# The left-over tokens' part of K^T V from two half tiles of 64 rows instead of one zero-padded tile of 128 rows

## The chip, the cores and the metric

The kernel runs on one core of a Trainium2 chip. The metric is the device time of one execution in microseconds (us). Four runs of the kernel before gave a median of 770.48 us (769.99 to 773.08). One execution was profiled: it took 770.82 us, of which 769.0 lie between the first and the last instruction of the program (the span).

The engines are named as in the profile: PE is TensorE's matmuls, PEld its weight loads, DVE is VectorE, ACT is ScalarE, POOL is GpSimd, SP is SyncE, which only issues transfers here. A q behind a name (SPq) is the engine's sequencer.

## The reference

A linear attention without softmax, a normalization, and a feed-forward block with a product of two projections, in float32:

```python
# q, k, v: (batch 8, heads 8, tokens 576, head_dim 64)
kv = np.einsum('bhsd,bhse->bhde', k, v)          # 64 x 64 for each batch and head
out = np.einsum('bhsd,bhde->bhse', q, kv)
rms = np.sqrt(np.mean(out * out, axis=-1, keepdims=True) + 1e-06)
x = (out / rms * g_norm)                          # then to (4608 tokens, 512)
a, b = x @ w1, x @ w2                             # 512 -> 1024 each
y = ((a * b) @ w3) @ w_out                        # 1024 -> 1024 -> 512
```

The change is in the first line alone: kv of one batch and head is a sum over 576 tokens.

## The kernel before

**Tokens.** 576 is four times 128 and 64 more. The kernel calls the 512 tokens G (J = 4 slices of P = 128) and the 64 tokens left over L. The 512 of each batch make one group of rows for the feed-forward block; the left-over tokens of all eight batches (8 x 64 = 512) make a ninth, so there are nine groups of 512 tokens.

**The stages.** First (about the first 88 us) the weights are read, converted, and w3 and w_out are folded into one matrix (L596 are the products of this, L583 the transposes), while the attention of batch 0 runs in between, one pair of heads at a time. Then nine groups follow: the gate products x@w1 and x@w2 (`gates`, Winograd's scheme with seven products, L617), and the output projection (`project` for the first group; `project_twice`, two levels of the scheme, L892, for the others). The attention of batch T+1 is spread over the gate products of group T: `winograd` calls `between()` twice for each of four blocks, so eight slots in a group, and `steps(b)` says what runs in each slot.

**Attention of a batch.** Heads are taken in pairs r = 0 to 3, heads 2r and 2r+1 (e = 0, 1). `kv(rs)` multiplies K^T and V for the pairs in rs. The result of head e lies on the PSUM partitions 64e to 64e+63 of one bank (`kv_ps`), 64 columns for each pair. For each pair there are J + 1 = 5 slices of the token sum: four of 128 tokens from the tiles `k_sb` and `v_sb`, and a fifth from the left-over tiles `kl_sb` and `vl_sb`. Each slice is two products (L326), one for each head, of 128 rows and 64 columns against 64 columns. A float32 product leaves two matmul records in the trace. Four copies of ACT (L337) then bring the bank to `kv_sb`, each head's block once to either half of the partitions. `product(h)` (L409) multiplies the queries of the pairs 2h and 2h+1 with kv: 32 products of 64 rows and 64 columns, with the row half (l) as the innermost loop and the column half (t) around it. `product_left` (L427) does the same for the left-over queries. `q_t` (L345) transposes queries on TensorE, in batch 0 and part of batch 1; later `q_by_dma` does it with transfers and POOL copies (L286, L288, L298).

**The left-over tiles.** `kv_left` holds two tiles, each of 128 partitions by 8 heads by 64. `load_kv_left(b)` (L105) fills partitions 0 to 63 with the 64 left-over tokens of batch b, one transfer each for k and v; partitions 64 to 127 are set to zero by POOL once, at the start (L250), and stay zero. There is one buffer: the rows of batch b+1 are loaded after the last pair of batch b has been multiplied.

**The order.** PE, POOL and SP issue in the order of the program text all the time (`manual_schedule`). DVE and ACT also do in the first stage, and DVE in the double projections; elsewhere their order is the framework's choice, by its own estimate of when each instruction is ready. SP's queue carries nearly all transfers, in order; a transfer whose buffer is still in use holds up those behind it. Transfers count on eight semaphores in turn, and one that takes a semaphore again waits for the transfer before it on the same one.

**Where it is called.** In batch 0, `begin(r)` runs `kv([r])` and `q_t(r)` for one pair in a block of the second half of the fold, four calls. For the other batches `begin_kv(0, 1)` and `begin_kv(2, 3)` run two pairs in one call, 14 calls:

```python
fs[1] += [(a.begin_kv, 2, 3), (a.finish, 0)]              # finish(h) runs product(h)
fs[second].append((batch(b + 1).begin_kv, 0, 1))
fs[second].append((a.finish, 1))
```

In batch 1 the call for pairs 0 and 1 is followed by `begin_q`, that is by L345. `begin_kv` issues after the products the loads of k and v two pairs ahead (`load_ahead`), and, behind those of the last pair, `load_kv_left(b + 1)`.

Of the kernel before, what the change touches and what calls it, by code (L numbers as in the profile page):

```python
# [11 lines left out]
FP32 = mybir.dt.float32  # L12
# [9 lines left out]
def kernel(  # L22
# [32 lines left out]
    nc = tc.nc  # L55
    PSUM = bass.MemoryType.PSUM
    P = 128

    B, H, S, D = q.shape
# [5 lines left out]
    J = 4  # L65
    G = J * P
    N = G // 2
    L = S - G
# [3 lines left out]
    const = ctx.enter_context(tc.tile_pool(name="const", bufs=1))  # L72
# [9 lines left out]
    def bank(pool, tag):  # L82
        return pool.tile([P, 512], FP32, name=tag, tag=tag)


    loaded = {}
    q_left = {}

    kv_left = [const.tile([P, H, D], FP32, name=f"{name}l_sb") for name in "kv"]

    def load_pair(names, b, r):

# [9 lines left out]

    def load_kv_left(b):
        for t, src in zip(kv_left, (k, v)):
            nc.sync.dma_start(out=t[0:L], in_=src[b, :, G:S, :].rearrange("h p d -> p h d"))  # L105

    def load_q_left(b):
        if b % 2 == 0:
# [137 lines left out]

    ident = const.tile([P, P], FP32, name="ident")
    make_identity(nc, ident)
    for t in kv_left:
        nc.gpsimd.memset(t[L:P], 0.0)  # L250
    eps_col = const.tile([P, 1], FP32, name="eps_col")
    nc.vector.memset(eps_col, 1e-6)

# [54 lines left out]
    def attention(b):  # L308
# [6 lines left out]
        def kv(rs):  # L315


            n = len(rs)
            kv_ps = bank(ps_at, "at")[:, 0:n * D].rearrange("p (r d) -> p r d", d=D)
            for r in rs:  # L320
                k_sb, v_sb = loaded["k", b, r], loaded["v", b, r]
                kl, vl = kv_left
                for j in range(J + 1):
                    cols = slice(j * D, (j + 1) * D)
                    for e in range(2):
                        nc.tensor.matmul(  # L326
                            kv_ps[e * D:(e + 1) * D, r - rs[0], :],
                            lhsT=k_sb[:, e, cols] if j < J else kl[:, 2 * r + e, :],
                            rhs=v_sb[:, e, cols] if j < J else vl[:, 2 * r + e, :],
                            start=(j == 0),  # L330
                            stop=(j == J),
                        )
            for e in range(2):
                for i in range(2):
                    dst = kv_b[i * D:(i + 1) * D, e, rs[0]:rs[0] + n, :]
                    src = kv_ps[e * D:(e + 1) * D]
                    nc.scalar.copy(dst, src)  # L337
# [130 lines left out]
        def load_ahead(names, r):  # L468

            if r + 2 < NP:  # L470
                load_pair(names, b, r + 2)
            elif b + 1 < B:
                load_pair(names, b + 1, r + 2 - NP)
                if r + 1 == NP and "k" in names:
                    load_kv_left(b + 1)

        def begin_kv(*rs):
            kv(rs)
            for r in rs:
                load_ahead("kv", r)  # L480
# [527 lines left out]
    with tc.manual_schedule(  # L1008
# [6 lines left out]
        for e in range(2):  # L1015
            nc.scalar.dma_start(
                out=g_row[:, e * D:(e + 1) * D], in_=g_norm.rearrange("(o d) -> o d", o=1)
# [13 lines left out]
        for c in range(KF):  # L1031

            if c == 0:
                end_next()
                begin_next()
            else:
                begin_next()
                end_next()
            if c == 4:
                load_kv_left(0)  # L1040
                load_pair("kvq", 0, 0)
            elif c == 5:
                load_pair("kvq", 0, 1)
                load_q_left(0)
            fold_chunk(0, c, range(NH - 1))
            turn_w3(*((0, c + 1) if c + 1 < KF else (1, 0)))
            fold_chunk(0, c, [NH - 1])
            if c == 0:
                keep_warm(4)
# [123 lines left out]
```

## Time and profile before

| what | value |
|---|---|
| median of four runs | 770.48 us |
| the profiled execution | 770.82 us, span 769.0 us |
| kv (L326) | 640 records, of them 128 from the left-over tiles |
| L409 and L427 | 1024 and 128 records |
| transfers | 132.55 MB, mean 172 GB/s |
| zeroing of the left-over tiles (L250) | 0.52 us for each of two |
| issue of the left-over tiles (L105) | 16 transfers, median 0.62 us each for k and 0.63 for v |

How to read the profile: the page gives busy time by engine, the share of each engine in the chain of work that ended last, and groups of instructions by line, "out<-in", shape, count, busy time, mean ns and the idle time before them. A matmul's own duration (222 ns for L326) is its way through the array; matmuls overlap, so what a group of them costs is read from starts, or from the chain in order of time, where each piece lasts until the next begins.

### The profile page before, as it was taken

The numbers are of one execution on the slowest core, as the hardware profiler recorded it, in microseconds if no ns is written. First come the engines' busy times: TensorE is split into PE (matmuls) and PEld (weight loads), VectorE is DVE, ScalarE is ACT, GpSimd is POOL, SyncE is SP. The second block draws the span as 40 slices with busy tenths as digits, with TensorE's granted clock in tenths as the row PEclk, the third lists the DMA queues.
The fourth block names the chain that finished last, engine by engine and source line by source line (L and its number), as shares of the span: only waits on it lengthen the run. The fifth ranks groups of instructions, "written<-read, shape, count | busy, mean of one in ns | idle before, by whom it ended". The sixth has DMA issues, their size and how long they took to land.

```text
span 769.0 us, 14423 instructions
## 1 busy us (share of the span) xinstructions
PE 759.1 (99%) x5775; PEld 659.3 (86%) x5775; DVE 543.0 (71%) x1087; ACT 249.9 (32%) x483; POOL 134.9 (18%) x132
## 2 busy tenths in 40 slices
PE   7999999999999999999999999999999999999997
PEld 5455788888899889988998899889988998898897
DVE  7978999438978577756775777658665863594566
ACT  6687743213322232223213322332233222212221
POOL 0000000122610451133114511340144000000000
PEclk9999999999999999999999999999999999999999
DMA  9995641338997854874486548744843460074015
GB/s 316 338 346 171 211 138 42 83 92 256 325 305 250 233 109 129 270 199 110 128 280 176 124 139 285 180 109 146 279 70 43 159 233 0 1 244 146 1 52 175
DMA packets 132776, 132.55 MB, mean 172 GB/s; under 512 B 76645, under 2 KB 120677, under 8 KB 132709
## 3 DMA queue, kind: packets, MB, share of 16 engines
q1 hardware_dynamic: 130256, 116.81, 52.3%
q10 hardware_dynamic: 2452, 14.81, 5.7%
q8 instruction: 46, 0.75, 0.4%
q14 instruction: 22, 0.17, 0.1%
HBM read 100.27 MB, written 16.38 MB: 152 GB/s over the span
## 4 chain that ended last, share of the span: by engine, by line
PE 93%; DMA 4%; ACT 2%; DVE 1%; issue 0%; SPq 0%; DVEq 0%; ACTq 0%
PE mm L617 60%; PE mm L892 21%; PE mm L596 6%; PE at L326 3%; PE at L409 2%; DMA raw<-in_moe_w_dram 1%; DMA raw<-in_moe_w_out_dram 1%; DMA raw<-w3o_l 1%; PE at L583 1%; PE at L345 0%; ACT ab L152 0%; ACT w_sb L153 0%; PE at L427 0%; DMA out_dram<-raw 0%; ACT w3o_sb L601 0%; PE at L442 0%
## 5 line engine op out<-in xcount | busy, mean ns | idle before, releaser
L617 PE MATMUL mm<-xT,w_sb 128*128 128x256 f32 x768 | 176.2, 379 | 0.0
L617 PEld LDWEIGHTS mm<-xT,w_sb 128*128 128x128 f32 x768 | 145.5, 190 | 19.9 <-issue 0.5
L617 PE MATMUL mm<-xc,ws 128*128 128x256 f32 x576 | 130.5, 379 | 0.3 <-ACT p L630 0.3
L617 PEld LDWEIGHTS mm<-xc,ws 128*128 128x128 f32 x576 | 109.4, 190 | 15.5 <-ACT p L630 0.7
L756 DVE TENSOR_TENSOR c<-mm,u 128x512 f32<-128x512 f32 x36 | 24.8, 689 | 105.7 <-PE mm L617 105.7
L630 ACT COPY u<-mm 128x512 f32<-128x512 f32 x74 | 43.3, 585 | 139.0 <-PE mm L617 128.8
L630 ACT COPY p<-mm 128x512 f32<-128x512 f32 x74 | 43.3, 586 | 84.5 <-PE mm L617 78.5
L617 PE MATMUL mm<-xc,w_sb 128*128 128x256 f32 x288 | 69.3, 383 | 0.0
L892 PE MATMUL mm<-w3o_sb,raw 128*128 128x128 f32 x500 | 62.3, 276 | 0.0
L596 PE MATMUL mm<-chunks,ab 128*128 128x512 f32 x128 | 60.2, 601 | 1.9 <-ACT chunks L153 1.3
L617 PE MATMUL mm<-xT,ws 128*128 128x256 f32 x256 | 61.1, 382 | 0.0
L284 POOL COPY xT<-xn 128x1024 uint16<-128x1024 uint16 x26 | 32.2, 1265 | 160.2 <-DVE xn L387 160.1
L617 PEld LDWEIGHTS mm<-xc,w_sb 128*128 128x128 f32 x288 | 53.7, 190 | 7.7 <-ACT u L630 0.2
L757 DVE TENSOR_TENSOR ab<-c 128x256 f32<-128x256 f32 x108 | 58.0, 537 | 3.0
L892 PEld LDWEIGHTS mm<-w3o_sb,raw 128*128 128x128 f32 x500 | 59.0, 192 | 0.1
L617 PEld LDWEIGHTS mm<-xT,ws 128*128 128x128 f32 x256 | 48.0, 190 | 6.6
L378 DVE TENSOR_REDUCE inv<-sq 128x8 f32<-128x512 f32 (+1 forms) x40 | 23.4, 625 | 35.2 <-ACT sq L377 35.2
L756 DVE TENSOR_TENSOR c<-p,u 128x512 f32<-128x512 f32 x36 | 28.2, 783 | 27.9 <-ACT u L630 27.7
L892 PE MATMUL mm<-w3o_sb,ab 128*128 128x128 f32 x336 | 43.7, 275 | 0.0
L903 ACT COPY u<-mm 128x512 f32<-128x512 f32 x23 | 13.5, 586 | 87.5 <-DVE raw L916 56.7
L596 PEld LDWEIGHTS mm<-chunks,ab 128*128 128x128 f32 x128 | 21.9, 190 | 22.9 <-issue 15.8
L892 PEld LDWEIGHTS mm<-w3o_sb,ab 128*128 128x128 f32 x336 | 41.0, 192 | 0.3
(157 smaller groups left out, 1135.0 us busy)
## 6 DMA issues: line engine op xcount, KB each, us to landing
w3o_sb<-w3o_l SPq DMA_DIRECT2D x26, 896.0 KB, 5.0
raw<-in_moe_w_dram SPq DMA_DIRECT2D x31, 512.0 KB, 7.3
raw<-w3o_l SPq DMA_DIRECT2D x13, 896.0 KB, 4.8
w3o_sb<-w3o_l ACTq DMA_DIRECT2D x11, 896.0 KB, 4.6
k_sb<-in_k_dram SPq DMA_DIRECT2D x32, 256.0 KB, 3.9
v_sb<-in_v_dram SPq DMA_DIRECT2D x32, 256.0 KB, 4.7
q_sb<-in_q_dram SPq DMA_DIRECT2D x32, 256.0 KB, 4.4
out_dram<-raw SPq DMA_DIRECT2D x14, 512.0 KB, 3.6
```

The costliest lines, as they stand in the source:

```text
L284: nc.gpsimd.tensor_copy(to, src.rearrange("p a n w -> p w a n"))
L326: nc.tensor.matmul(kv_ps[e * D:(e + 1) * D, r - rs[0], :], lhsT=k_sb[:, e, cols] if j < J else kl[:, 2 * r + e, :], rhs=v_sb[:, e, cols] i ...
L378: nc.vector.tensor_reduce(out=inv[:, i], in_=sq.rearrange("p (h d) -> p h d", d=D), axis=AX.X, op=ALU.add)
L409: nc.tensor.matmul(o_ps[l][tokens, n * D:(n + 1) * D], lhsT=qT[r][rows, e, i, tokens], rhs=kv_b[rows, e, r, :], start=True, stop=True,)
L583: nc.tensor.transpose(t_ps[:, m, :], src, ident)
L596: nc.tensor.matmul(sums_ps[half][m], lhsT=w3T[half, c][:, m, :], rhs=chunks[:, c, 1, :], start=(c == 0), stop=(c == KF - 1),)
L617: nc.tensor.matmul(ps[:, u, :], lhsT=lhsT(a_name, u, c), rhs=rhs(b_name, c),  start=(u == 0 and c == 0 and to is None), stop=(c == chunks ...
L630: nc.scalar.copy(t, ps)
L756: nc.vector.tensor_add(c, one, two)
L757: nc.vector.tensor_mul(dst, c[:, 0, :], c[:, 1, :])
L892: nc.tensor.matmul(to[:, i, :], lhsT=x[:, c, :], rhs=y[:, c, :], start=new and place // 4 not in seen, stop=(c == 1), skip_group_check=True,)
L903: nc.scalar.copy(t[:, 0:4], ps[0])
```

## The change

The left-over tiles get 4 heads instead of 8 in each partition: heads 0 to 3 (pairs 0 and 1) lie on partitions 0 to 63, heads 4 to 7 (pairs 2 and 3) on partitions 64 to 127. Nothing is zero, so the two memsets go. `load_kv_left` issues two transfers for each of k and v, one for each half. The products of the left-over tokens use 64 rows instead of 128: both heads of a pair, and both pairs of a call, take the same half of the rows. In `kv` all slices of 128 tokens of all pairs of the call come first, then the left-over products of all pairs. The start flag of the accumulation is set only for the first pair's first slice (for each head) instead of for each pair's first slice, and the stop flag on the left-over products.

```diff
-    kv_left = [const.tile([P, H, D], FP32, name=f"{name}l_sb") for name in "kv"]
+    kv_left = [const.tile([P, H // 2, D], FP32, name=f"{name}l_sb") for name in "kv"]
...
     def load_kv_left(b):
         for t, src in zip(kv_left, (k, v)):
-            nc.sync.dma_start(out=t[0:L], in_=src[b, :, G:S, :].rearrange("h p d -> p h d"))
+            for i in range(2):
+                heads = src[b, i * H // 2:(i + 1) * H // 2, G:S, :]
+                nc.sync.dma_start(out=t[i * L:(i + 1) * L], in_=heads.rearrange("h p d -> p h d"))
...
-    for t in kv_left:
-        nc.gpsimd.memset(t[L:P], 0.0)
...
+            def add(r, e, k_in, v_in, start, stop):
+                nc.tensor.matmul(
+                    kv_ps[e * D:(e + 1) * D, r - rs[0], :], lhsT=k_in, rhs=v_in,
+                    start=start, stop=stop, skip_group_check=True,
+                )
+
             for r in rs:
-                k_sb, v_sb = loaded["k", b, r], loaded["v", b, r]
-                kl, vl = kv_left
-                for j in range(J + 1):
-                    cols = slice(j * D, (j + 1) * D)
+                for j in range(J):
                     for e in range(2):
-                        nc.tensor.matmul(
-                            kv_ps[e * D:(e + 1) * D, r - rs[0], :],
-                            lhsT=k_sb[:, e, cols] if j < J else kl[:, 2 * r + e, :],
-                            rhs=v_sb[:, e, cols] if j < J else vl[:, 2 * r + e, :],
-                            start=(j == 0),
-                            stop=(j == J),
-                        )
+                        k_in, v_in = (loaded[name, b, r][:, e, j * D:(j + 1) * D] for name in "kv")
+
+                        add(r, e, k_in, v_in, r == rs[0] and j == 0, False)
+
+            for r in rs:
+                rows = slice(r // 2 * L, (r // 2 + 1) * L)
+                for e in range(2):
+                    k_in, v_in = (t[rows, r % 2 * 2 + e, :] for t in kv_left)
+                    add(r, e, k_in, v_in, False, True)
```

## The prediction

> **What bounds the kernel now.** First the shares of the page, then the chain of work that ended last, because the bound of a stage is what ends last there.
>
> ```profile
> PE 759.1 (99%) x5775; PEld 659.3 (86%) x5775; DVE 543.0 (71%) x1087; ACT 249.9 (32%) x483; POOL 134.9 (18%) x132
> ...
> PE 93%; DMA 4%; ACT 2%; DVE 1%; issue 0%; SPq 0%; DVEq 0%; ACTq 0%
> ```
>
> TensorE is busy for 99% of the span and carries 93% of the chain; its granted clock reads 9 tenths or more in all 40 slices. Other work costs time only where TensorE waits for it. So the question is how long TensorE needs for the changed products, and whether anything else becomes late. The chain in order of time gives that (start, length, what; x counts records, and one float32 product leaves two):
>
> ```profile
> 64.30 0.73 PE at L326 x20
> 65.03 0.59 PE at L345 x4
> ...
> 69.49 0.76 PE at L326 x20
> 70.25 0.02 issue
> 70.27 0.20 ACT kv_sb L337
> ...
> 102.17 1.32 PE at L326 x40
> 103.49 1.02 PE at L345 x8
> 104.51 5.18 PE mm L617 x24
> ...
> 138.70 1.31 PE at L326 x40
> 140.02 1.09 PE at L409 x64
> ...
> 153.39 0.62 PE at L427 x32
> ...
> 178.39 1.32 PE at L326 x40
> ...
> 199.99 1.31 PE at L326 x40
> 201.30 1.09 PE at L409 x64
> 202.39 19.19 PE mm L617 x88
> ```
>
> L326 is kv. 20 records take 0.73 us and 40 take 1.31, so one record costs 0.029 us and a group pays 0.15 us beyond its records (0.73 - 20 x 0.029). L409 and L427 are the 64x64 products with kv: 64 records take 1.09 and 32 take 0.62, which is 0.0147 us a record, again with 0.15 fixed. L345, the 128x128 transposes after kv: (1.02 - 0.59)/4 = 0.11 a record, 0.15 fixed. L617 has 0.2158 a record where no other shape stood just before (5.18/24); behind L409, 88 records take 19.19 instead of 18.99, so 0.20 fixed. I read the fixed part as what a change of tile shape costs, 0.15 to 0.20 us each. Then the shapes themselves and the left-over rows:
>
> ```profile
> L326 PE MATMUL at<-v_sb,k_sb 128*64 128x64 f32 x512 | 20.6, 226 | 0.0
> L409 PE MATMUL at<-kv_sb,qT 64*64 64x64 f32 x1024 | 18.6, 221 | 0.0
> ...
> L326 PE MATMUL at<-vl_sb,kl_sb 128*64 128x64 f32 x128 | 9.2, 222 | 0.0
> ```
>
> The last line is what the change remakes: 128 records of 128 rows by 64 columns, half of the rows zero. At 0.029 they are 3.7 us of the span, the most that the edit of the products could ever save.
>
> **The change part by part.** The sum is made against the profiled execution: 769.0 us of span and 1.8 around it, 770.82, which is 0.34 above the median 770.48 of the four runs.
>
> *Products of the left-over rows.* Still 128 records, now 64 rows by 64 columns. In a call of kv both pairs of heads use the same half of the rows (pairs 0 and 1 the lower, 2 and 3 the upper); only the two heads of a pair lie in different column halves. The trace has no such group, so I bound it. L409 puts four tiles side by side (two row halves by two column halves) at 0.0147 a record, which is 4 records per 0.0587 us; kv now puts two column halves side by side, 2 records per 0.058. The new group has two tiles, as kv has, so I take 0.029 a record: no gain. From below: the rate of L409, 128 x (0.029 - 0.0147) = 1.8 us saved. From above: the two tiles after each other, 0.058 a record, 128 x 0.029 = 3.7 us lost.
>
> The Trainium skill, TensorEngine Tiling (Array Packing), section Performance Considerations, asks for row tiling where the contraction is at most 64, and its Overview puts the speedup at up to 2x. By that the 128 records would cost 1.85 us less and the sum would end about 1.0 us below the time before. The same page's Key Properties says that changing the tiling mode drains TensorE, which speaks against the change and agrees with the 0.15 to 0.20 us above.
>
> *Changes of shape.* In 13 of the 18 calls of kv, all from 109.69 on, kv is followed by L409, as at 138.70 and 199.99. There the order 128x128, 128x64, 64x64, 128x128 stays; the change to 64x64 only moves ahead of the left-over products. Nothing is added. In batch 0 the four calls run one pair each, and kv is followed by the 128x128 transposes L345 (at 47.80, 52.99, 64.30 and 69.49); so it is at 102.17. Five calls get one change of shape more: 0.15 us into 64x64, and 0 to 0.05 more on the way back (0.20 instead of 0.15). That is 0.75 to 0.95 us, all on the chain: the chain stays on TensorE from 15.66 to 70.25, and at 70.27 the chain goes on through the kv copies, which wait for the last left-over product. I take +0.85. From below it is 0, if the fixed part belongs to the 128-row shapes alone; L427, 64x64 right behind L617 with the same 0.15, speaks against that.
>
> *Order inside kv.* The left-over products of the first pair now wait for the second pair's k and v too; these landed long before (issued a half batch ahead), and the copies to kv_sb wait for the whole bank in both versions. Nothing. A call now waits for its own half of the left-over rows: two landings per call instead of two per batch. The calls at 178.39 and 199.99, without and with such a wait, took 1.32 and 1.31, so the waits cost nothing.
>
> *Transfers.* Each batch issues four transfers for the left-over rows instead of two, each with half the pieces and the same bytes in all. First the view of the tile (ns, least/median/most of one issue), then SP's rows in order of time:
>
> ```profile
> L105 SPq DMA_DIRECT2D kl_sb<-in_k_dram x8: 607/616/749, 27.5 to 484.8; - x8
> ```
>
> ```profile
> 70.15 0.37 SPq L95 DMA_DIRECT2D k_sb<-in_k_dram  x1
> ...
> 71.13 0.62 SPq L105 DMA_DIRECT2D kl_sb<-in_k_dram  x1
> 71.80 0.63 SPq L105 DMA_DIRECT2D vl_sb<-in_v_dram  x1
> ```
>
> 512 pieces (64 rows by 8 heads) take SP 0.62 us, the 256 of k_sb 0.37. A half has 256 pieces: 0.37. So SP works 4 x 0.37 + 2 x 0.05 - 2 x 0.62, about 0.35 us more per batch; from above, with 0.62 for a half, 1.3 us; from below nothing. Behind it on SP's queue: once (73.85) the loads of the last weights, else the transposes of q for the pairs 2 and 3. Those had landed at 193.5 in the batch around 200, POOL had qT ready at 195.4, and TensorE read it at 201.23: 5.8 us to spare. The left-over rows themselves landed at 191.25 and are read from 199.99 on: 8.7 us to spare. The weight loads are on the chain: issued from 73.85 on, they land at 82.17, 83.68, 85.13, 86.48, 87.84, every 1.4 us, while SP issues the first ones 0.5 to 0.6 apart. They queue behind data, not behind SP, so I cost the later issue at nothing; without that cover it is 0.35, at most 1.3.
>
> The Trainium skill, DMA: Bandwidth & Descriptors, Rules for kernel authors, advises against two transfers to disjoint halves of the partitions, since both are spread over the same engines, and says that under 64 KB one pays mostly overhead; a half here is 64 KB. With the page's fixed 2.0 us for each of the 16 added transfers on the path it would be an estimate of 32 us more; the slack above says that they are not on the path.
>
> *The two memsets* of POOL go (0.52 us each, at 1.0 and 1.96). One stands between the two steps that build the identity, so the warm-up matmuls start up to 0.5 us earlier. The chain begins with weight transfers and ACT until 15.66, so nothing comes of it.
>
> Sum: +0.85, from the median 770.48 to 771.3. With the issue time on the chain and its upper price, 0.95 + 1.3, it would be 772.7; with no change of shape paid, 770.5. A measurement of this kernel can tell about 0.3% (2.3 us) from no change: 768.2 to 772.8 is the same.
>
> **The rivals.**
>
> *The planner sets another order (slower).* From the first gate product on, the order on DVE and ACT is not written out but chosen by the framework from its own estimates of when each instruction is ready. Other products and more transfers can swap neighbours. For it: DVE is at 9 tenths from 77 to 134 us, and TensorE once already waits for a bank (at 88.02, 0.28 us, its weight load 0.68, for the copy p of L630). Against it: that is nearly the only such wait, five banks buffer, and nothing that DVE or ACT do is changed. One such wait of 0.28 to 0.68 in each of nine groups is 2.5 to 6.1; with 0.37, 3.3, so 774.6. It decides from about four of the longer ones.
>
> *The two heads of a pair don't run side by side on half of the rows (slower).* At L326's left-over records, +3.7: 775.0 with the changes of shape. It decides once a record takes more than 0.040 us (1.45 us more than the sum). Against it: L409's four tiles include two that share rows.
>
> *The left-over products run beside L409 (faster).* They share the shape now, and L409 also uses the other row half. Fully hidden they give 3.7 - 0.85 = 2.85 us, 767.6; at L409's rate 1.0, so 769.5. Against it: L409 keeps both halves busy in turn, so a half that is taken by kv delays it by as much.
>
> *Nothing moves*: the extra shape changes hide behind the weights' transfers of the first 88 us: 770.5.
>
> **How the numbers follow.** As summed 0.48 (own range 770.4 to 772.7); nothing moves 0.05; beside L409 0.08, of which 0.05 is below 768.2; planner 0.31; not side by side 0.08. Faster 0.05, same 0.48 + 0.05 + 0.03 = 0.56, slower 0.39. The range goes from 769.3 (below it lies the deeper part of the faster case, some 0.06) to 775.3 (above it a part of the planner's, some 0.09).
>
> **What would show it.** Right: the chain's L326 groups as x32 with x8 of the left-over tile at 0.03 us a record; the group before L409 at 1.3 us with L409 at about 0.95 (its fixed part moved into L326), their sum 2.40 as now; the calls of batch 0 longer by 0.15 to 0.20; L105 sixteen times per tensor at about 0.37; TensorE's idle time unchanged. Wrong: a sum of 2.3 or 2.6 there; new idle time of TensorE before L617 with DVE or ACT as releaser; weights that land later than 82 us by more than TensorE's own delay.

## The result and the profile after

The changed kernel takes 772.13 us (median of 51 runs; 770.36 for 79 runs of the kernel before, measured beside it). The medians differ by 1.77 us. The ratio of the two over all these runs is 1.0019, with a 95% interval of 1.0013 to 1.0025, or 1.46 us more (1.0 to 1.9); this is the figure used below. By the bound of 0.3% this is the same; the interval leaves no doubt that it is a little slower. The profiled execution has a span of 770.1 us (769.0 before).

The page of the kernel after, busy time of the engines and their shares of the chain of work that ended last:

```profile
PE 760.8 (99%) x5775; PEld 660.6 (86%) x5775; DVE 542.4 (70%) x1087; ACT 249.7 (32%) x483; POOL 134.0 (17%) x130
...
PE 96%; DMA 2%; DVE 1%; ACT 1%; issue 0%; SPq 0%; DVEq 0%; ACTq 0%
```

The same number of matmul records, TensorE still the bound, two POOL instructions fewer (the memsets). The chain in order of time (start, length, what); all line numbers have moved (kv by minus five, the others by plus five), so kv is now L321, the transposes behind it L350, the products with kv L414, the gate products L622 and their copies L635:

```profile
65.37 0.88 PE at L321 x20
66.25 0.59 PE at L350 x4
...
87.39 1.06 ACT w3o_sb L606 x2
88.46 1.05 ACT w_sb L155
89.50 0.48 ACT p L635
...
90.03 14.21 PE mm L622 x64
104.24 1.46 PE at L321 x40
...
202.12 1.39 PE at L321 x37
203.51 0.06 PE at L414 x2
...
203.58 0.93 PE at L414 x62
204.51 19.19 PE mm L622 x88
```

Three things can be read here. A call of batch 0 takes 0.88 us instead of 0.73, and the call of batch 1 that stands in front of transposes 1.46 instead of 1.32. In the steady state kv and L414 together go from 202.12 to 204.51, 2.39 us, where they took 2.40 (199.99 to 202.39): nothing. And in front of the gate product at 90.03 the chain runs over ACT, from 87.39 on. In the kernel before it had left TensorE at this place too, and for longer, from 70.27 to 88.02, by way of SP's issue of the last weights and their transfer (before):

```profile
73.90 0.52 SPq L190
...
74.48 7.69 DMA raw<-in_moe_w_dram
...
82.25 1.16 ACT ab L152
...
87.49 0.48 ACT p L630
...
88.02 14.15 PE mm L617 x64
```

So already before the change SP's issue of these weights stood on the way to the gate product at 88.02.

I set every matmul record of this trace against the record of the same number in the trace of before; the difference of their starts (the offset) shows where time comes in. From the first record of kv to the first one behind kv, or behind L409 where that follows, it grows by this much (us; the times are those of before):

| kernel | 48 | 53 | 64 | 69 | 102 | 110 | each of the 12 calls from 139 on |
|---|---|---|---|---|---|---|---|
| changed | 0.14 | 0.15 | 0.14 | 0.14 | 0.14 | -0.06 | -0.01 to -0.02 |

The calls of batch 0 and the one at 102 sum to 0.71, the 13 others to -0.2: there the offset rises by 0.15 at the first left-over record and falls again at the first record of L414. Apart from the calls it jumps by 0.65 at the gate product that starts at 90.03. Together 1.2, inside the measured 1.0 to 1.9. Three more steps are in the trace, +0.75 by 15.66 us, +0.3 between 222 and 240, and -1.08 at 687. The first and the last are landings of weights that differ between executions: the twelve later profiles stand between -0.2 and +0.6 at 15.66, and all but one of them win the same 1.08 at 687, where the profile of before had waited 0.9 us for a transfer. The step at 222 to 240 is as large in the kernel with the order alone changed (+0.34, third experiment below), which ends no slower than the kernel before.

What comes late at 90 us starts on SP. The timeline of the kernel after (start, length, engine, line, operation, in brackets the idle time ahead and what ended it):

```profile
72.30 1.30 SPq L107 DMA_DIRECT2D kl_sb<-in_k_dram  x2
73.64 1.27 SPq L107 DMA_DIRECT2D vl_sb<-in_v_dram  x2
...
76.31 12.14 SPq L192 DMA_DIRECT2D raw<-in_moe_w_dram  x8
...
84.34 1.13 ACT L154 ACTIVATE ab<-raw 128x1024 f32<-128x1024 uint32 x1 [1.45 <-DMA raw<-in_moe_w_dram]
...
90.03 1.99 PE L622 MATMUL mm<-xc,ws 128*128 128x256 f32 x8 [0.93 <-ACT p L635]
```

The four transfers occupy SP for 2.61 us (72.30 to 74.91) where two took 1.30. The weights' loads start at 76.31 instead of 73.85, the second one lands at 84.26 instead of 82.17, and ACT, which works in order, waits 1.45 us for it (0.72 before). The copy p that TensorE needs stands behind three such conversions. TensorE waits 0.93 us for it instead of 0.28.

The left-over products by shape, and the issues of one left-over tile (ns: least, median, most):

```profile
L321 PE MATMUL at<-vl_sb,kl_sb 64*64 64x64 f32 x128 | 7.6, 232 | 0.0
...
L107 SPq DMA_DIRECT2D kl_sb<-in_k_dram x16: 595/602/755, 28.6 to 487.9; - x16
```

A half tile takes SP 0.60 us, as long as the whole one did (0.62).

### The profile page after: what moved, and what is told of

The parts are those of the page before. It is cut to its first block, busy times and chain, and to the rows that moved or that the text cites. A ratio compares the mean times of both kernels' runs of the same rounds, so it can differ in the third digit from the quotient of the medians.

```text
span 770.1 us, 14435 instructions
## 1 busy us (share of the span) xinstructions
PE 760.8 (99%) x5775; PEld 660.6 (86%) x5775; DVE 542.4 (70%) x1087; ACT 249.7 (32%) x483; POOL 134.0 (17%) x130
## 4 chain that ended last, share of the span: by engine, by line
PE 96%; DMA 2%; DVE 1%; ACT 1%; issue 0%; SPq 0%; DVEq 0%; ACTq 0%
PE mm L622 60%; PE mm L897 22%; PE mm L601 7%; PE at L321 3%; PE at L414 2%; DMA raw<-in_moe_w_out_dram 1%; PE at L588 1%; PE at L350 1%; DMA raw<-in_moe_w_dram 0%; PE at L447 0%; PE at L432 0%; DMA out_dram<-raw 0%; ACT ab L154 0%; DVE raw L921 0%; ACT w3o_sb L606 0%; ACT w_sb L155 0%
## 5 line engine op out<-in xcount | busy, mean ns | idle before, releaser
L622 PE MATMUL mm<-xT,w_sb 128*128 128x256 f32 x768 | 176.2, 379 | 0.0
L622 PEld LDWEIGHTS mm<-xT,w_sb 128*128 128x128 f32 x768 | 145.5, 190 | 19.9 <-issue 0.5
L622 PE MATMUL mm<-xc,ws 128*128 128x256 f32 x576 | 130.5, 379 | 0.9 <-ACT p L635 0.9
L622 PEld LDWEIGHTS mm<-xc,ws 128*128 128x128 f32 x576 | 109.4, 190 | 16.1 <-ACT p L635 1.3
L635 ACT COPY u<-mm 128x512 f32<-128x512 f32 x74 | 43.3, 586 | 137.9 <-PE mm L622 131.0
L635 ACT COPY p<-mm 128x512 f32<-128x512 f32 x74 | 43.3, 585 | 84.5 <-PE mm L622 81.1
L622 PE MATMUL mm<-xc,w_sb 128*128 128x256 f32 x288 | 69.3, 383 | 0.0
L622 PE MATMUL mm<-xT,ws 128*128 128x256 f32 x256 | 61.1, 382 | 0.0
L622 PEld LDWEIGHTS mm<-xc,w_sb 128*128 128x128 f32 x288 | 53.7, 190 | 7.8 <-ACT u L635 0.3
L622 PEld LDWEIGHTS mm<-xT,ws 128*128 128x128 f32 x256 | 48.0, 190 | 6.6
L761 DVE TENSOR_TENSOR c<-p,u 128x512 f32<-128x512 f32 x36 | 26.5, 735 | 27.1 <-ACT u L635 27.1
```

The costliest lines, as they stand in the source:

```text
L622: nc.tensor.matmul(ps[:, u, :], lhsT=lhsT(a_name, u, c), rhs=rhs(b_name, c),  start=(u == 0 and c == 0 and to is None), stop=(c == chunks ...
L635: nc.scalar.copy(t, ps)
L761: nc.vector.tensor_add(c, one, two)
```

## The experiments

The theory after this reading: 0.71 us are five changes of tile shape, 0.65 are SP's time in front of the last weights, the rest of the change is free. The rivals: that the products themselves or their order cost, that weights wait for data and not for SP, and that the framework's order on DVE and ACT has shifted. The last one needed no run: the instructions on ACT and on DVE of the two compiled kernels follow each other in the same order, one by one.

### Transfers alone, products alone

The kernel before with four transfers, everything else untouched:

```diff
-            nc.sync.dma_start(out=t[0:L], in_=src[b, :, G:S, :].rearrange("h p d -> p h d"))
+            for i in range(2):
+                heads = src[b, i * H // 2:(i + 1) * H // 2, G:S, :]
+                nc.sync.dma_start(
+                    out=t[0:L, i * H // 2:(i + 1) * H // 2, :], in_=heads.rearrange("h p d -> p h d")
+                )
```

> The kernel before, with one change: the left-over rows of k and v come in two transfers each (heads 0 to 3, heads 4 to 7) instead of one. Products, zeros and memsets stay. Theory (transfers make the last weights late): a half takes SP about 0.60 us to issue, so SP is 1.2 to 1.3 us later at the loads of the last weights (73.85 in the kernel before); they land 0.7 to 1.3 us later than in the kernel before, TensorE waits longer before the gate products that begin at 88.02, and the whole is 0.5 to 0.9 us longer (ratio about 1.0009). Rival (the weights queue behind data, not behind SP, as predicted): landing unchanged, ratio 1.0000 within its interval.

Measured: 1.0010 (0.9995 to 1.0024). The halves take 0.60 to 0.61 us; the weights' loads start at 75.28 instead of 73.85, the second lands at 82.94 instead of 82.17, and the offset of the matmul records grows by 0.51 at 88.02 and at no call of kv. The trace says what was expected; the interval alone would not decide.

The changed kernel with the two transfers and the zeros of before; all heads stay on partitions 0 to 63:

```diff
-                    k_in, v_in = (t[rows, r % 2 * 2 + e, :] for t in kv_left)
+                    k_in, v_in = (t[0:L, 2 * r + e, :] for t in kv_left)
```

> The changed kernel, with the two transfers and the memsets of the kernel before: all eight heads' left-over rows on partitions 0 to 63, and all left-over products on those 64 rows; order and shapes as in the changed kernel. Theory: only the five added changes of shape remain, 5 x 0.145 = 0.7 us, ratio about 1.0009; the groups of kv in batch 0 take 0.88 instead of 0.73 us, the weights land as in the kernel before plus TensorE's own delay of up to 0.6. Rival (the wait before 90.03 in the changed kernel comes from the products, not from the transfers): about +1.4 us, ratio 1.0018, as the changed kernel.

Measured: 1.0012 (1.0004 to 1.0021). The offset grows by 0.14 to 0.15 at each of the five calls in front of transposes and by nothing at the others, as in the changed kernel, and at 88.02 it falls by 0.44 instead of growing, for here the weights landed early (80.89). The interval alone still holds the rival's 1.0018; the trace has no wait at 88. So the two parts cost about as much each, and the wait at 88 belongs to the transfers; how firmly, the comparison of all profiles below tells.

### Is it the order inside a call?

The kernel before with the changed loops alone (all slices of 128 tokens first, then the left-over products, still 128 rows with zeros):

```diff
-                    k_in, v_in = (t[rows, r % 2 * 2 + e, :] for t in kv_left)
+                    k_in, v_in = (t[:, 2 * r + e, :] for t in kv_left)
```

> The kernel before with the changed order of the products alone: in a call all slices of 128 tokens of all pairs first, then the left-over products of all pairs, still of 128 rows with zeros, from the tiles and transfers of before. Theory (the order costs nothing): no offset at any call of kv, ratio 1.0000, taken as 0.9995 to 1.0005. Rival (part of what the 64-row products seemed to cost in the run with the products alone is the order, which makes the first pair's last products wait): some 0.14 us at each of the calls of batch 0 or at each two-pair call, 0.6 to 2 us, ratio 1.0008 to 1.0026.

Measured: 0.9997 (0.9988 to 1.0006). The offset grows by 0.00 at 17 of the 18 calls (-0.04 at 110). The order is free.

### What does a change of shape cost?

The kernel before with 64 rows in place, behind each pair's own slices:

```diff
-                            lhsT=k_sb[:, e, cols] if j < J else kl[:, 2 * r + e, :],
-                            rhs=v_sb[:, e, cols] if j < J else vl[:, 2 * r + e, :],
+                            lhsT=k_sb[:, e, cols] if j < J else kl[0:L, 2 * r + e, :],
+                            rhs=v_sb[:, e, cols] if j < J else vl[0:L, 2 * r + e, :],
```

> The kernel before, with the left-over products reading 64 rows, but left where they stand: behind each pair's own four slices, so that a call of two pairs goes 128x64, 64x64, 128x64, 64x64. Same tiles, same two transfers per batch, zeros kept and not read. Theory (a change of shape costs 0.145 us, whatever stands around it): 13 calls in front of L409 get two changes more each (3.77), the call at 102 three (0.44), the four calls of batch 0 one each (0.58): 4.8 us, ratio 1.0062, taken as 1.0055 to 1.0070. Rival (the 0.145 us seen at the first left-over record are not the change of shape but a cost of the 64-row products, which ends as soon as other 64-row products follow): the same 128 records in the same calls, 0.7 to 1.5 us, ratio 1.0009 to 1.0020.

Measured: 1.0055 (1.0042 to 1.0068); 4.6 us between the medians. The chain of this kernel at the call that took 1.31 + 1.09 before:

```profile
201.51 1.70 PE at L326 x38
...
203.26 0.93 PE at L409 x61
204.20 1.93 PE mm L617 x8
```

From 201.51 to 204.20 are 2.69 us instead of 2.40: two changes of shape more, 0.145 each. The offset grows by 0.14 to 0.15 in each call of batch 0, by 0.44 at 102 and by 0.28 at each of the 12 calls from 139 on. So it is the change that costs, not the 64-row product, and the price is the same in every place.

### Does the steady state pay?

The change from batch 2 on; batches 0 and 1 keep tiles, zeros, two transfers and 128 rows:

```diff
+                    if b < 2:
+                        k_in, v_in = (t[:, 2 * r + e, :] for t in kv_left)
+                    else:
+                        k_in, v_in = (t[rows, r % 2 * 2 + e, :] for t in kv_left)
```

> The change from batch 2 on alone. Batches 0 and 1 have the left-over rows as before (two transfers, 128 rows, the zeros written at the start), in the changed order of the products; batches 2 to 7 have four transfers of half tiles and 64-row products on either half of the rows. Theory (the whole cost lies in the five calls in front of the transposes and in batch 1's transfers in front of the last weights; in the steady state the change of shape only moves and the transfers are hidden): +0.15 us in kv and -0.15 us in L409 at each call from 125 us on, ratio 1.0000, taken as 0.9995 to 1.0004. Rival (each batch pays something that two profiles can't show): 12 of the 18 calls carry two thirds of the 1.46 us, ratio 1.0013.

Measured: 1.0006 (0.9990 to 1.0023), medians 770.36 and 770.49. The interval is too wide to shut out the rival. The trace does it for the calls: over each of the 12 changed ones the offset moves by -0.01 to -0.02, and TensorE waits for none of the left-over tiles. One wait is new, 0.66 us at 469 us for weights of the output projection (`w3o_sb`). The changed kernel has no such wait there, and kernels with two transfers have one like it at 546 to 549 us (0.56 to 0.76), so it can't be put down to the change.

### Does SP stand in front of the weights?

More transfers in this one place alone, in the kernel before:

```diff
+            cuts = [0, 3, 6, H] if b == 1 else [0, H]
+            for i, j in zip(cuts, cuts[1:]):
+                hs = slice(i, j)
+                nc.sync.dma_start(out=t[0:L, hs], in_=src[b, hs, G:S, :].rearrange("h p d -> p h d"))
```

> The kernel before, with the left-over rows of batch 1 alone brought by six transfers instead of two (three for each tensor: 3, 3 and 2 heads, all to partitions 0 to 63). All products and all other batches are as before. At 0.60 us an issue, SP reaches the last weights' loads 2.4 us later: first issue at about 76.3 instead of 73.85, as in the changed kernel, but with TensorE itself not late. Theory (SP's issue time stands in front of the weights, and they on the chain): the second load lands at about 84.3 instead of 82.17, and the gate products at 88.02 start 1.3 to 1.9 us later, because nothing else has used up the slack; nothing more after that. Ratio 1.0017 to 1.0025. Rival (the prediction's cover: the weights queue behind data, not behind SP): landing of the later weights unchanged, ratio 1.0000.

Measured: 1.0027 (1.0016 to 1.0038). SP in this kernel, and what TensorE waited for (us in total, times, longest):

```profile
71.03 1.98 SPq L108 DMA_DIRECT2D kl_sb<-in_k_dram  x3
73.05 1.91 SPq L108 DMA_DIRECT2D vl_sb<-in_v_dram  x3
...
76.37 11.40 SPq L193 DMA_DIRECT2D raw<-in_moe_w_dram  x8
...
PE mm L620 <- ACT p L633: 1.7, 1, 1.7
```

The second load lands at 83.58 and the offset grows by 1.38 us at the gate products. That is inside the expected range, and the rival (1.0000) is out. "Nothing more after that" was a miss: a second wait, 1.5 us at 227, has another cause (last section).

All profiles in which batch 1's left-over rows are issued ahead of these weights, set side by side (us). The landing of the second load is taken less TensorE's own offset at 80 us, so that a kernel that is late as a whole does not count as late weights:

| transfers of batch 1 | profiles | SP's time for them | second load lands | TensorE waits at the first gate products |
|---|---|---|---|---|
| two | 8 | 1.30 | 80.2 to 82.2, mean 81.0 | once 0.28, the others under 0.2 |
| four | 3 | 2.61 | 81.5 to 82.9, mean 82.4 | 0.78 to 0.93 |
| six | 1 | 3.93 | 83.6 | 1.66 |

The mean landing moves by what SP works longer, 1.4 and 2.6 us for 1.3 and 2.6. And the one profile of two transfers in which TensorE waits is that of the kernel before. Against it the four transfers of the changed kernel cost 0.65. In the seven others the offset falls by 0.55 just behind 88.02, and in three of them it rises again at the next gate products, by 0.36 at most; against these the four transfers cost 0.8 to 1.2.

### Taking SP's time away: two misses

Batch 1's left-over transfers behind the last weights instead of in front of them, first in the changed kernel, then in the kernel before:

```diff
-                if r + 1 == NP and "k" in names:
+                if r + 1 == NP and "k" in names and b:
...
                 for _ in range(3):
                     load_next()
+                load_kv_left(1)
```

> The changed kernel, with the four transfers of batch 1's left-over rows (and no others) issued behind the last weights' loads instead of ahead of them. Theory: SP reaches the weights about 2.6 us earlier than in the changed kernel, they land earlier than in the kernel before, and the time falls by at least the 0.7 us of the transfers, to +0.7 or less against the kernel before (ratio 1.0009 or below; down to 1.0003 if the kernel before itself waits for these weights). Rival (TensorE's wait at 90.03 has another cause): stays at +1.4, ratio 1.0018.

> The kernel before, with the two transfers of batch 1's left-over rows issued behind the last weights' loads. Theory: SP reaches the weights about 1.3 us earlier, ACT's wait of 0.72 us for them at 82.25 and TensorE's 0.28 (weight load 0.68) at 88.02 shrink, so 0.2 to 0.6 us faster than the kernel before, ratio 0.9993 to 0.9997. Rival (the loads are bound by when their buffers come free or by the data ahead of them): ratio 1.0000.

Measured: 1.0036 (1.0023 to 1.0049) and 1.0025 (1.0013 to 1.0036), slower than both theories had said. The weights did land earlier: their conversion on ACT starts at 80.56 and 79.58 us instead of 82.25. But the framework, which orders ACT and DVE by its own estimate, has now put two conversions ahead of the copies that TensorE needs, most likely because it expects the weights earlier. ACT and TensorE in the second of the two kernels:

```profile
79.58 1.15 ACT L152 ACTIVATE ab<-raw 128x1024 f32<-128x1024 uint32 x1 [0.90 <-DMA raw<-in_moe_w_dram]
80.63 1.18 ACT L153 ACTIVATE w_sb<-raw 128x1024 f32<-128x1024 f32 x1
81.72 0.56 ACT L588 COPY ab<-at 128x512 f32<-128x512 f32 x1
...
82.33 3.70 PE L596 MATMUL mm<-chunks,ab 128*128 128x512 f32 x8 [0.93 <-ACT ab L588]
```

and ACT in the kernel before, where the copy comes first:

```profile
79.02 0.59 ACT L588 COPY ab<-at 128x512 f32<-128x512 f32 x1 [0.88 <-PE at L583]
...
80.45 1.07 ACT L444 COPY xT<-at 128x512 f32<-128x512 f32 x2 [0.85 <-PE at L442]
...
82.25 1.16 ACT L152 ACTIVATE ab<-raw 128x1024 f32<-128x1024 uint32 x1 [0.72 <-DMA raw<-in_moe_w_dram]
```

The prediction's rival of another order, which the change itself did not cause, costs 1.1 to 1.9 us at this product as soon as the transfers are moved. So these two runs say nothing on SP's time; the run with six transfers, whose order on ACT and DVE is that of before, does.

### The memsets

```diff
+    for n in range(2):
+        nc.gpsimd.memset(w3o_sb[L:P, n, :], 0.0)
```

> The changed kernel with POOL's work at the start put back: two memsets of 64x512 at the place of the old ones, on rows of w3o_sb that are overwritten later. Theory (the memsets are hidden; what the profile of the changed kernel shows up to 15.66 us is the first weights landing late by chance): warm-up matmuls 0.6 us later again, the first fold products where the weights put them, ratio to the kernel before as the changed kernel's, 1.0019, taken as 1.0010 to 1.0027. Rival (the earlier identity is what costs 0.75 us up to 15.66): ratio 1.0009.

Measured: 1.0015 (1.0003 to 1.0027). The interval holds both 1.0019 and the rival's 1.0009. The traces tell more: with the memsets the first fold products start 0.04 us later than before, without them 0.75 (changed kernel) and 0.16 later (the first kernel of the section above, which has no memsets either), and 0.56 in the second one of that section, which has them. So the 0.75 is no effect of the earlier identity.

### Can the left-over products be faster at all?

Both heads and both pairs of a call use one half of the rows. Here pair r lies on the half r mod 2. The Trainium skill, TensorEngine Tiling (Array Packing), Restrictions and Gotchas, says that different row tiles must write to different PSUM banks; L409 does so (one bank for each row half). No run here shows what one bank would do. So each pair gets its own bank:

```diff
+            banks = [bank(ps_at, "at"), bank(ps_mm, "mm")] if two else [bank(ps_at, "at")] * 2
...
-                rows = slice(r // 2 * L, (r // 2 + 1) * L)
-                for e in range(2):
+            for e in range(2):
+                for r in rs:
+                    rows = slice(r % 2 * L, (r % 2 + 1) * L)
```

> The layout of before for batches 0 and 1; from batch 2 on the two pairs of a call take different halves of the rows: pair r lies on the half r mod 2 (eight transfers per batch, one for each pair and tensor), the left-over products run with the pair as the inner loop, and each pair has its own PSUM bank (the second one from the pool of the gate products), so ACT makes eight half-wide copies to kv_sb instead of four. Theory (the change gains nothing in the products because both heads of a pair use one half of the rows, and two tiles side by side are all that a record of 128x64 had too; with all four tiles side by side the rate of L409, 0.0147 us a record, is reached): kv with L409 behind it takes 2.28 us instead of 2.40 in each of 12 calls, 1.4 us in all, ratio 0.9982, if the copies and banks stay hidden. Rival 1 (the rate does not depend on the half of the rows): still 2.40, ratio 1.0000. Rival 2 (the borrowed bank or the added copies make TensorE wait): a wait of 0.3 to 0.6 us before L617 or L409 in each of the 12 calls, ratio 1.003 to 1.008.

Measured: 1.0076 (1.0054 to 1.0097). The theory was right on the products (the offset falls by 0.12 over each of the 12 calls) and the price was paid elsewhere, though not by bank or copies as rival 2 had it: the eight transfers hold up the transposes of q behind them.

```profile
259.10 2.68 SPq L112 DMA_DIRECT2D kl_sb<-in_k_dram  x4
261.84 2.56 SPq L112 DMA_DIRECT2D vl_sb<-in_v_dram  x4
...
267.20 1.27 SPq L295 DMA_TRANSPOSE ql_sb<-qT_left  x1
...
272.00 0.79 PE L449 MATMUL at<-kv_sb,qT_left 64*64 64x64 f32 x32 [1.82 <-POOL qT_left L305]
```

This wait comes twice (272 and 427 us, 1.8 and 1.9). Another, 1.5 us at 214, is for a copy of ACT and leads back over DVE and POOL to a transpose of x; DVE has another order shortly before, so the share of each is open. And the first wait cost more than its length: behind it the granted clock reads 0.50 from 274 to 276 us, gate products take 0.43 us a record instead of 0.216, and some 1.8 us more are lost. Behind the second, no shorter, the clock stayed at 1.00.

So the transfers were issued later, in two parts:

```diff
+            if more:
+                fs[2].append((load_kv_left, b + 1, (0, 1)))
+                fs[3].append((load_kv_left, b + 1, (2, 3)))
```

> As the run with both halves of the rows, but the eight transfers of the left-over rows of batches 2 to 7 are issued later and in two parts: four (pairs 0 and 1) one slot behind the products that free the tiles, four (pairs 2 and 3) two slots behind, both behind the transposes of q and before the first call that reads them. Theory (the products gain 0.11 to 0.12 us in each of 12 calls, and what was lost came from 5.2 us of SP in front of the transposes of q): the two waits of 1.9 us before L427 and the one of 1.5 us before L617 are gone, kv with L409 behind it stays at 2.29 us, ratio 0.9982, taken as 0.9970 to 1.0000. Rival (the borrowed bank and the added copies of ACT, or another order on DVE between the gate products and the double projection, cost as much): ratio 1.0010 to 1.0030, with waits of TensorE for ACT or DVE in the trace.

Measured: 1.0064 (1.0037 to 1.0090). The waits before the left-over queries are gone, and from 255 us on the offset falls by 0.12 over each call and grows by little between them. All was lost between 195 and 241 us, where SP also moves the folded matrix: TensorE waits 0.7 us for ACT at 198, 1.9 for a transfer of that matrix at 233 and 0.6 for DVE at 236. Again the clock adds to it: it reads 0.50 from 234 to 240 us, which is 2.5 to 3 of the 5.5 us lost between 222 and 241. The chain there:

```profile
215.13 4.22 SPq L295
...
219.40 11.55 DMA xn<-xT
...
231.06 2.25 POOL xT L305 x2
```

The transposes of x come late. The order on DVE is another one there too, so which share each has in the waits stays open. The last run avoids both by starting at batch 4:

```diff
-            two = b >= 2
+            two = b >= 4
...
-            if more:
+            if more and b > 2:
```

> The version with both halves of the rows and the later transfers, but only for batches 4 to 7; batches 0 to 3 have the tiles, the two transfers, the place of the transfers and the 128-row products of the kernel before (in the changed order inside a call). So nothing is added to SP's queue before 330 us, and the order on ACT and DVE is that of before but for the copies to kv_sb. Theory (each of the 8 calls left gains 0.117 us, and what ate it in the last run lay between 195 and 240 us, in SP's queue and on DVE): 0.94 us less than before, ratio 0.9988, taken as 0.9975 to 1.0000; kv with L409 behind it 2.29 us from 330 us on and no new wait of TensorE. Rival (the borrowed bank, the copies or the transfers make TensorE wait in the steady state too): ratio 1.0005 to 1.0030.

Measured: 0.9986 (0.9978 to 0.9995), medians 769.18 and 770.28. This is faster than the kernel before, by 1.1 us of 770 (0.4 to 1.7), and the rival is out. The offset falls by 0.12 over each of the 8 calls, 0.9 in all. At the calls at 102, 139, 178, 200 and 254, which still have 128 rows, it grows by 0.05; there the pair is the inner loop too, so that two products in a row use the same columns. That this is the reason is argued, not shown; a version without it wasn't tried. Nor were the two banks without the two row halves, or the halves without the banks: the gain is shown for both together. The chain at a call:

```profile
330.36 0.61 PE at L330 x16
330.98 0.47 PE mm L330 x16
331.44 0.20 PE at L330
...
331.72 0.93 PE at L431 x64
332.65 19.19 PE mm L642 x88
```

kv and the products with kv take 2.29 us (330.36 to 332.65) instead of 2.40.

## Why the prediction was right or wrong

**The time.** 771.3 was predicted, +0.85 on the time before; +1.46 was measured. The direction of the sum, the range and "the same by 0.3%" held. The sum was short by 0.6. One term was missing, and it is larger than that: the shape changes came out 0.14 below what was summed, and the steady calls gave back 0.2 that the sum didn't have. That these two partly covered for the missing term is luck.

**Products of the left-over rows: right.** 0.029 us a record, no gain. The steady calls show it (2.39 against 2.40), and the run with both row halves supports the reason that the prediction gave: two tiles side by side before and after. The speedup that the Trainium skill promises for row tiling (the prediction's citation) is there once both halves of the rows work at the same time, each in its own bank, 0.12 us in a call of eight such records, and not before.

**Changes of shape: right, a little high.** Taken at 0.85 for five calls, measured 0.71 in the trace: 0.14 to 0.15 each. The run with the changes inside the call confirms the price at every call.

**Order inside kv, memsets: right.** Nothing, by the run with the order alone and by the traces with and without memsets.

**Transfers: this step failed.** "A half has 256 pieces: 0.37" was read from a tile of 128 partitions; a half of 64 partitions takes 0.60, so the upper price (1.3 us of SP per batch) was the true one. And "they queue behind data, not behind SP, so I cost the later issue at nothing" was wrong for the first weights: their landing moved by 2.09 us when TensorE itself was only 1.36 us late, the very sign that the prediction had named as one against it. The 1.4 to 1.5 us between two landings are there before and after (82.17 and 83.68, then 84.26 and 85.74), but the whole row moves with SP's issue. The chain of before had SP's issue in it (73.90, shown above), in rows that the prediction's excerpt skips. Between the landing and TensorE stands ACT, with little slack: 1.31 us of SP became 0.65 us of TensorE against the profile of before, in which ACT already waited 0.72 for these weights and TensorE 0.28 for ACT, and 0.8 to 1.2 against the profiles that did not wait. With 0.71 for the shapes and -0.2 for the steady calls that is 1.2 to 1.7, around the measured 1.46. With the bounds given (0.35 to 1.3) the sum would have been 1.2 to 2.2. For all other batches the cover named, 5.8 us of slack before the q transposes are read, held.

**The rivals.** The planner's order didn't change, but the two misses show how near it was. The two heads do run side by side. Left-over products beside L409: two to four records of L414 start ahead of the last left-over one, worth 0.01 to 0.02 us in most calls.

## What to carry to other kernels

A smaller tile saves TensorE nothing if the other half of the rows stays empty: count the tiles that work at the same time, and count the changes of shape, 0.145 us each here. A transfer cut in two costs the queue twice its issue time, and a cover that holds in seven batches must be looked at in the eighth, where something that the end waits for stands behind it. Before transfers are moved on a queue, look at what a planner will make of the new times.

## What the hardware showed that I had not expected

**Issue time did not go by the number of pieces.** On SP, transfers to the 64 partitions of the left-over tiles took 0.62 us with 8 heads (512 pieces) and 0.60 to 0.62 with 4, 3 or 2 (256 to 128 pieces); transfers of 256 pieces to 128 partitions (k_sb, v_sb, q_sb) took 0.39 to 0.47 (all medians). The pieces of the two kinds also differ in length, 256 bytes and 1 KB, so whether the partitions or the length set the time is not shown. The Trainium skill, DMA: Bandwidth & Descriptors, Rules for kernel authors, advises against two transfers to disjoint halves; the direction agrees, though what they cost here was SP's time to issue them, 2.61 us instead of 1.30.

**POOL's copies stretch DVE's instructions.** The run with six transfers lost 1.5 us at 227 us. POOL and DVE there, and TensorE's wait:

```profile
223.91 2.58 POOL L301 COPY xT<-xn 128x1024 uint16<-128x1024 uint16 x2 [10.70 <-DMA xn<-xT]
...
224.11 1.38 DVE L674 TENSOR_TENSOR raw<-raw,ab 128x256 f32<-128x256 f32 x1
225.41 1.36 DVE L674 TENSOR_TENSOR ab<-ab 128x256 f32<-128x256 f32 x1
226.70 0.41 DVE L857 TENSOR_TENSOR ab<-ab 128x256 f32<-128x256 f32 x1
...
PE mm L895 <- DVE ab L857: 1.5, 1, 1.5
```

and in the kernel before:

```profile
225.27 2.47 POOL L298 COPY xT<-xn 128x1024 uint16<-128x1024 uint16 x2 [13.08 <-DMA xn<-xT]
...
225.80 0.93 DVE L671 TENSOR_TENSOR raw<-ab,raw 128x256 f32<-128x256 f32 x1
226.65 1.37 DVE L850 TENSOR_TENSOR inner_sums<-raw 128x256 f32<-128x256 f32 x1
```

While POOL makes its two copies, two instructions of DVE take up to 1.38 us instead of 0.42. In the kernel before, they are two that nobody waits for yet; with the gate products and POOL shifted they are the two in front of the sum that TensorE waits for. The stretching is no accident of this place: in the kernel before, 49 operations of DVE on two tiles of 128x256, none with an input from PSUM, meet such a copy of POOL and take 1.14 us in the median; 563 that meet none take 0.42. The Trainium skill, SBUF — State Buffer, section SBUF: two separate sides, says that DVE and GpSimd share a pair of ports that one of them holds for a whole instruction; the durations agree. So a shift of a microsecond can cost or save another one at a place where nothing was changed, and single profiles differ by that.
